# Blocks 1 and 2 of a fused attention and gated-MLP kernel: the place of scores, softmax and pooling inside a slot

## The chip, the cores and the metric

One core of one Trainium2 chip runs the whole kernel. The metric is the device time of one execution in microseconds (us): 1782.89 us as the median of three runs before the change (1781.92, 1782.89 and 1783.45).

## The reference, cut to what matters

The kernel chains three stages over 4608 tokens (8 batches of 576), all in float32 accuracy:

```python
k_p, v_p = mean of k and v over 8 neighbouring rows          # 72 pooled rows per head
attn = softmax(q @ k_p.T / sqrt(64))                          # 8 heads of 64 columns
x = attn @ v_p                                                # 4608 x 512
x = (silu(x @ w_gate) * (x @ w_val)) @ w_out                  # hidden width 1536
h = x @ w_in                                                  # hidden width 2048
out = (rational function of h, 4 + 2 coefficients) @ w_out2   # 4608 x 512
```

A product of two float32 matrices is made of three products of a high and a low part; that is the group of 12 matmuls (4 row tiles times 3) met below.

## The kernel before, in words

**Blocks and slots.** The tokens are cut into nine blocks of 512. Blocks 0, 1 and 2 go through the first layer one at a time (the loop `for j in range(PLAIN)` at L780); blocks 3 to 8 follow in three pairs (the loop at L911), and the second layer comes last. Within a block, a loop over f = 0 to 11 takes 128 hidden columns at a time. One pass of it is called a slot here; slot 7 of block 2 is j = 2, f = 7. In each slot TensorE (PE) makes a gate product `gp` and a value product `vp` (12 matmuls of 128x512 each), ScalarE (ACT) takes the Silu of `gp` (L803), and VectorE (DVE) multiplies it with `vp` (L817), which frees the bank of `vp`.

**Attention rides along.** While block j is in its first layer, the attention of a later block is computed in the same slots. Attention is cut into units of up to 128 tokens, one or two of which form a group. `attention_slots` (L486) writes a plan: for each unit a list of functions with a slot and a place in the slot; `place` (L710) runs those of one place. A unit goes through these steps, named by letters here:
- Q: load of its queries on SP's DMA queue (L276).
- S: scores, 16 small matmuls (L372) into two PSUM banks.
- M: `soft1`, on DVE: maximum and subtraction for each of the two banks (L380, L383), into the tile `p`.
- E: `soft_exp`, one ACT exponential in place (L393). Exp and Silu need different function tables on ACT, so each change between them shows an ACT_TABLE_LOAD.
- N: `soft2` and `soft3`: sum, reciprocal on DVE (L405 to L407), multiplication of `p` (L408: on POOL where `helped` is set, which holds for the units of the pairs; on DVE for the four units of block 2), and two copies on POOL into the tile `pr` (L416).
- T: `transposes`, 6 small transposes on PE (L433, L437), then two copies on ACT (`evac`: L440, L441) and a subtraction on DVE (`evac_low`, L445).
- V: `values`, once for each group, 8 to 12 small matmuls on PE (L461, L464), then two copies on ACT (L470). Where the next group belongs to another batch, `build_vs` follows (L318: two POOL products, an ACT copy at L336, a POOL subtraction).

The tile `p` has two buffers and `pr` one. The units of block 2 have S in slots 4 to 7 of block 1; the nine units of the pair of blocks 3 and 4 have S in slot 11 of block 1 and slots 0 to 7 of block 2. V falls into slots 6, 8 and 9 of block 1 and slots 2, 4, 5, 7 and 9 of block 2. The first unit of the next pair has S in slot 11 of block 2.

**Other work in the slots.** `prepare` (L692) loads two pieces of k or v of a coming batch and returns `run`, which pools the pieces loaded a slot earlier with one DVE reduction each (L291, L309). `sum_weights` (even slots: two DVE additions, L640, and four POOL operations) and `sum_splits` (odd slots: two ACT copies, two DVE subtractions, L94) make sums of first-layer weights that the pairs will use; `sum_store` (L653) writes them and two original tiles to DRAM with four DMAs. In block 2, `second` (class `Halves`, L180) converts a piece of the second layer's weights in each of slots 1, 3, 5, 7 and 9: `begin` stores what the turn before made, loads, and runs two ACT instructions (L117, L118); `middle` runs two on DVE (L127, L121) and one on POOL (L124); `end` runs one on ACT (L97) and one on POOL (L101). `stream` (L739) loads weight tiles for the pairs; `token_sums` (L717) makes eight DVE subtractions in slot 10 of block 2, and `token_part` splits a tile on ACT and DVE for the first products of the pairs (`ca`, `cc`, `cb`).

**What sets the order.** Each engine runs its instructions in the order in which the program writes them, which is set by hand here; waits between engines follow the data and the buffers. DMAs of these stages go through one queue, SP's. The order in one slot of blocks 1 and 2 before the change is: place "0" (M and E of the unit whose scores came in the slot before); loads of k and v; `second.begin`; `sum_weights`; `gp`, Silu; place "A" (T); `sum_splits`, `sum_store`; `vp`; `second.middle`; `run`; place "B" (N, then V); multiplication L817; place "B2" (Q of the next unit), `store_plain`; `second.end`; place "C" (S).

```python
            put(slot, "C", ... scores(u, ...))
            put(slot + 1, "0", lambda u=u: box["s", u][0]())            # M, then E
            put(slot + 1, "B", lambda u=u: [fn() for fn in ...[2:]])    # N
            put(slot + 2, "A", t_)                                      # T
                put(slot + 2, "B", v_)                                  # V
```

Of the kernel before, what the change touches and what calls it, by code (L numbers as in the profile page):

```python
# [20 lines left out]
B, H, S, D = 8, 8, 576, 64  # L21
# [12 lines left out]
PLAIN = 3  # L34
# [30 lines left out]
def attention_gated_rational(  # L65
# [413 lines left out]
    def qload(u, early=False, eng=None):  # L479
        b, s, n, o = u  # L480
        off = NPAIR * (b * S + s)
        return at_load(q[:, off : off + NPAIR * n], f"q{b}_{s}", early, NPAIR * n, eng)
# [3 lines left out]
    def attention_slots(js, start, helped=False, heads=False):  # L486


        def put(slot, place, fn):
            plan.setdefault((slot, place), []).append(fn)  # L490

        groups = [g for j in js for g in units(j)]
        owner = [j for j in js for g in units(j)]
        box = {}
        fl = [(g, i) for g in range(len(groups)) for i in range(len(groups[g]))]

        def do_xraw(j):
            if j > PLAIN and (j - PLAIN) % 2:
                st["xraw", j] = [wslot(f"xraw{j}_{i}", (P, 2, BLK), F32) for i in range(2)]
            else:  # L500
                t = keep.tile([P, KT, BLK], F32, tag="xraw", name=f"xraw{j}")
                st["xraw", j] = [t[:, 0:2, :], t[:, 2:4, :]]
        for n, (g, i) in enumerate(fl):
            u = groups[g][i]
            slot = start + n
            put(slot - 1, "B2", lambda u=u: box.__setitem__(("q", u), qload(u)))
            plain = NF1 <= slot < PLAIN * NF1 - 1
            at_bank = 2 if plain else None
            put(slot, "C", lambda u=u, at_bank=at_bank: box.__setitem__(
                ("s", u), scores(u, box.pop(("q", u)), False, helped, heads, at_bank)))  # L510
            put(slot + 1, "A0" if slot + 1 >= PLAIN * NF1 else "0", lambda u=u: box["s", u][0]())
            put(slot + 1, "0" if heads or plain else "A", lambda u=u: box["s", u][1]())
            put(slot + 1, "B" if slot >= NF1 else "B2", lambda u=u: [fn() for fn in box.pop(("s", u))[2:]])

            def t_(u=u, g=g, i=i, at_bank=0 if slot + 2 >= PLAIN * NF1 else None):
                if i == 0:
                    box["pt", g] = new_pt(f"{js[0]}_{g}")
                for fn in transposes(u, box["pt", g], i * P, at_bank):
                    fn()
            put(slot + 2, "A", t_)  # L520
            if i + 1 == len(groups[g]):
                def v_(g=g):
                    j = owner[g]
                    if ("xraw", j) not in st:
                        do_xraw(j)
                    values(groups[g], box.pop(("pt", g)), st["xraw", j])
                    if g + 1 < len(groups) and groups[g + 1][0][0] != groups[g][0][0]:
                        build_vs(groups[g + 1][0][0])
                put(slot + 2, "B", v_)
# [105 lines left out]
    def sum_weights(f):  # L635

        r = wslot(f"rs{f}", (P, 2, 2, QUART), F32)
        rg, rv = sums_w[f] = [r[:, i] for i in range(2)]
        for r, w in zip((rg, rv), (W1[f"g{f}"], W1[f"v{f}"])):
            nc.vector.tensor_tensor(r.rearrange("p h c -> p (h c)"), f32(w[:, 0, :]), f32(w[:, 1, :]), op=ALU.add)  # L640
        (a11, a12), (a21, a22) = ([r[:, h] for h in range(2)] for r in (rg, rv))
        nc.gpsimd.tensor_tensor(a11, a11, a21, op=ALU.subtract)
        nc.gpsimd.tensor_tensor(a21, a21, a22, op=ALU.add)
        nc.gpsimd.tensor_tensor(a22, a22, a11, op=ALU.subtract)
        nc.gpsimd.tensor_tensor(a12, a12, a22, op=ALU.subtract)
# [7 lines left out]
    def sum_store(f):  # L653
        for i, w in enumerate(sums_w.pop(f)):
            nc.sync.dma_start(s_d[f][i], f32(w))
        nc.sync.dma_start(w_d[f], f32(W1[f"g{f}"]))
        nc.sync.dma_start(v_d[f], f32(W1[f"v{f}"][:, :, QUART:]))
# [52 lines left out]
    def place(stage, f, p_):  # L710
        for fn in plan.pop((stage * NF1 + f, p_), []):
            fn()
# [47 lines left out]
    def store_plain(slot):  # L760
        j, f = slot // NF1 + 1, slot % NF1
        nc.sync.dma_start(h_d[0, f][:, j - 1, :], h2[j, f // 2][:, f % 2, :])
# [10 lines left out]
    def turns(n):  # L773

        if n < 0:
            return n % 2 if n > -NF1 and n < -1 else 0
        p, f = divmod(n, NF1)
        return (2 if 1 <= f < NF1 - 2 else 1) if n < 2 * NF1 else (2 if 1 <= f < 9 else int(f == 0))

    for j in range(PLAIN):  # L780
        for f in range(NF1):
            slot = (j - 1) * NF1 + f
            place(j, f, "0")
            if (j, f) in begin:
                todo += prep_jobs(begin[j, f])
            run = prepare(2, j > 0)
            if j == 2:
                second.begin(turns(f - NF1), turns(f - NF1 + 1))
            if j and slot % 2 == 0:
                sum_weights(slot // 2)  # L790
            g_w, v_w = W1[f"g{f}"], W1[f"v{f}"]
            if j == 0:
                first.step(6)
            pool, tag = (ps_acc, "acc") if j == 2 and f >= NF1 - 2 else (ps_gv, "gv")
            gp = pool.tile([P, BLK], F32, tag=tag, name=f"gp{j}_{f}")
            mm3(gp, [(g_w, slice(kk * P, (kk + 1) * P), x[kk], full) for kk in range(KT)], order=LOW_LAST)
            if j == 0:
                hh = hp.tile([P, BLK], F32, tag="hh", name=f"hh{j}_{f}", bufs=2)
            else:
                if f % 2 == 0:  # L800
                    h2[j, f // 2] = wslot(f"hh{j}_{f}", (P, 2, BLK), F32)
                hh = h2[j, f // 2][:, f % 2, :]
            nc.scalar.activation(hh, gp, AF.Silu)  # L803
            place(j, f, "A")
            if j == 0:
                first.step(6)
            if j and slot % 2:
                sum_splits(slot // 2)
            if slot > 0 and slot % 2 == 0:
                sum_store(slot // 2 - 1)  # L810
            vps = pool.tile([P, BLK], F32, tag=tag, name=f"vp{j}_{f}")
            mm3(vps, [(v_w, slice(kk * P, (kk + 1) * P), x[kk], full) for kk in range(KT)], order=LOW_LAST)
            if j == 2:
                second.middle()
            run()
            place(j, f, "B")
            nc.vector.tensor_tensor(hh, hh, vps, op=ALU.mult)  # L817
            if j == 0:
                ht = hp.tile([P, 2, BLK], F32R, tag="ht", name=f"ht{j}_{f}", bufs=2)
                nc.scalar.activation(ht[:, 0, :], hh, AF.Copy)  # L820
                first.step(6)
                low_part(ht[:, 1, :], hh, ht[:, 0, :])
                h_t[f] = ht
            place(j, f, "B2")
            if j and slot % 2 == 0 and slot:
                store_plain(slot - 2)
                store_plain(slot - 1)
            if j == 0 and f:
                out_mm(f - 1)
            if j == 2:  # L830
                second.end()
            place(j, f, "C")
            if j == 1 and f == NF1 - 2:
                nxt, convs = convert_x(st.pop(("xraw", 2)), "x2", True)
                for c_ in convs:
                    c_()
            if j == 2 and f == NF1 - 4:
                stream(0, 1, 0)
            if j == 2 and f == NF1 - 3:
                stream(0, 2, 3)  # L840
            if j == 2 and f == NF1 - 2:
                token_sums(0, nc.vector)
                stream(1, 1, 0)
                token_part(0, "b11")
        if j == 0:
            first.finish()
            nxt, convs = convert_x(st.pop(("xraw", 1)), "x1")
            for c_ in convs:
                c_()
            out_mm(NF1 - 1)  # L850
            ys = halves(keep.tile([P, KT, BLK], F32, tag="xraw", name="ys0"))
            for i in range(KT):
                nc.scalar.activation(ys[i // 2][:, i % 2, :], acc[i], AF.Copy)
            for i in range(2):
                nc.sync.dma_start(y_dram[0][:, 2 * i : 2 * i + 2, :], ys[i])
        x = nxt
# [50 lines left out]
    token_part(0, "t1")  # L907
    begin_chain(0)
    token_part(0, "t2")
    stream(1, 2)  # L910
    for n in range(full_n):  # L911
        p, f = divmod(n, NF1)
        stage = PLAIN + p
# [342 lines left out]
```

## Time and profile before

| | us |
|---|---|
| median of three runs | 1782.89 |
| the profiled execution | 1778.77 |
| its span, first to last instruction | 1777.0 |
| block 1, slots 0 to 4 up to slot 4's S: ten products and nothing else on PE | 157.31 to 184.60 |
| block 1, from the first S to slot 11's S | 184.60 to 243.04 |
| block 2, up to the end of its last `vp` | 243.04 to 348.60 |

Busy shares of the span: PE 97%, DVE 79%, ACT 64%, POOL 17%; the mean granted TensorE clock is 0.997 of full speed. Times below are us from the span's start. In a timeline row, the bracket gives the time that the engine sat idle before the instruction and what released it; a row "x12" merges twelve instructions. Ends of matmuls are modelled, and a row's length holds the drain of its last one, so durations in a chain are taken from start to start where the next row allows it.

### The profile page before, as it was taken

Reading aid. Unit: us, or ns where it says so; the run is one execution under the profiler, and the core shown is the slowest. Engines: PE = TensorE matmul, PEld = TensorE weight load, DVE = VectorE, ACT = ScalarE, POOL = GpSimd, SP = SyncE. Lnnn points to the kernel's source line nnn. Section 1 sums busy time; section 2 is a strip of 40 time slices with the busy share of each in tenths; the row PEclk is TensorE's granted clock in tenths of the full one; section 3 lists DMA queues with packets and bytes.
Section 4 is the critical chain, followed back from the end, with each engine's and each line's share of the span. In section 5 each row is a group of like instructions: output and inputs, shape, how many; then the busy total and the mean of one; then the engine's idle time right before and its main releaser. Section 6 shows DMA issues by size and latency. Waiting matters only on the chain.

```text
span 1777.0 us, 23705 instructions
## 1 busy us (share of the span) xinstructions
PE 1729.2 (97%) x8176; PEld 1417.5 (80%) x8176; DVE 1403.9 (79%) x2303; ACT 1145.1 (64%) x2014; POOL 294.2 (17%) x396
## 2 busy tenths in 40 slices
PE   6999899899999999999999999999999999999999
PEld 5777677678877888878888888888888888888887
DVE  7995666668786654377777899989898989898987
ACT  6794455477676754355545677777777777777775
POOL 3443234325535542100000000000000000000000
PEclk9999999999999999999999999999999999999999
DMA  7834655799999999996417601000000000000000
GB/s 291 295 127 157 237 187 210 279 351 365 387 325 355 338 346 346 394 384 230 161 64 259 226 7 42 25 24 25 24 25 24 25 24 25 24 25 24 1 24 25
DMA packets 132505, 297.87 MB, mean 168 GB/s; under 512 B 12960, under 2 KB 54560, under 8 KB 131360
## 3 DMA queue, kind: packets, MB, share of 16 engines
q1 hardware_dynamic: 131520, 295.75, 45.7%
q8 instruction: 65, 1.06, 0.2%
q10 hardware_dynamic: 864, 0.60, 0.1%
q14 instruction: 56, 0.46, 0.1%
HBM read 200.87 MB, written 95.42 MB: 167 GB/s over the span
## 4 chain that ended last, share of the span: by engine, by line
PE 81%; DVE 7%; ACT 6%; DMA 3%; issue 2%; POOL 2%; SPq 0%; DVEq 0%; POOLq 0%; ACTq 0%
PE acco L260 22%; PE h L260 22%; PE ca L260 10%; PE ya L1099 7%; PE cc L260 5%; PE yc L1099 4%; PE cb L260 2%; PE vp L260 2%; PE yb L1099 2%; PE gp L260 2%; PE pv L461 1%; PE sc L372 1%; ACT L803 1%; DMA sw<-sd 1%; DVE p L383 1%
## 5 line engine op out<-in xcount | busy, mean ns | idle before, releaser
L260 PE MATMUL h<-z,wi 128*128 128x512 f32 x1728 | 414.6, 389 | 0.0
L260 PE MATMUL acco<-wo,gt 128*128 128x512 f32 x1728 | 414.6, 389 | 0.0
L260 PEld LDWEIGHTS h<-z,wi 128*128 128x128 f32 x1728 | 324.5, 188 | 67.2
L260 PEld LDWEIGHTS acco<-wo,gt 128*128 128x128 f32 x1728 | 324.4, 188 | 67.2
L1165 ACT ACTIVATE sq<-h 128x512 f32<-128x512 f32 x144 | 85.8, 596 | 175.3 <-PE h L260 175.3
L1172 DVE SCALAR_TENSOR_TENSOR w<-sq,neg,w 128x512 f32<-128x512 f32 x144 | 107.9, 749 | 43.0 <-ACT w L1166 42.9
L1182 DVE SCALAR_TENSOR_TENSOR g<-t,neg,e 128x512 f32<-128x512 f32 x144 | 108.3, 752 | 5.1
L1186 ACT ACTIVATE gt<-g 128x512 fp32r<-128x512 f32 x144 | 90.9, 631 | 32.8 <-DVE g L1182 32.8
L1169 ACT ACTIVATE t<-h,neg 128x512 f32<-128x512 f32 x144 | 111.8, 776 | 0.0
L1178 DVE SCALAR_TENSOR_TENSOR t<-t,neg,h 128x512 f32<-128x512 f32 x144 | 107.7, 748 | 5.1
L260 PE MATMUL gp<-x,wg 128*128 128x512 f32 x432 | 109.5, 401 | 0.8 <-DVE wg L94 0.8
L260 PE MATMUL vp<-x,wv 128*128 128x512 f32 x432 | 109.3, 400 | 0.7 <-DVE wv L94 0.4
L1179 DVE SCALAR_TENSOR_TENSOR e<-w,ln 128x512 f32<-128x512 f32 x144 | 98.6, 685 | 13.5 <-ACT ln L1176 13.5
L1176 ACT ACTIVATE ln<-ln,lnb 128x512 f32<-128x512 f32 x144 | 104.3, 724 | 4.7
L1166 ACT ACTIVATE w<-h,cab 128x512 f32<-128x512 f32 x144 | 98.5, 684 | 8.2 <-DVE e L1179 8.1
L1180 DVE SCALAR_TENSOR_TENSOR e<-e,ln 128x512 f32<-128x512 f32 x144 | 99.7, 692 | 5.0
L1187 DVE TENSOR_TENSOR gt<-g,gt 128x512 fp32r<-128x512 f32 x144 | 98.9, 687 | 2.2 <-ACT gt L1186 0.8
L1177 DVE TENSOR_TENSOR t<-t,h 128x512 f32<-128x512 f32 x144 | 98.2, 682 | 0.0
L260 PEld LDWEIGHTS vp<-x,wv 128*128 128x128 f32 x432 | 80.6, 191 | 19.7 <-DVE wv L94 2.8
L260 PEld LDWEIGHTS gp<-x,wg 128*128 128x128 f32 x432 | 80.1, 190 | 20.4 <-DVE wg L94 2.9
L1175 ACT ACTIVATE ln<-w 128x512 f32<-128x512 f32 x144 | 91.5, 635 | 0.1
L930 DVE TENSOR_TENSOR cc<-cq,ca 128x512 f32<-128x512 f32 x36 | 25.0, 694 | 58.9 <-PE ca L260 58.9
(262 smaller groups left out, 3167.1 us busy)
## 6 DMA issues: line engine op xcount, KB each, us to landing
sw<-sd SPq DMA_DIRECT2D x72, 512.0 KB, 7.0
sw<-wd SPq DMA_DIRECT2D x36, 512.0 KB, 6.8
h<-hq SPq DMA_DIRECT2D x36, 512.0 KB, 7.0
sd<-ws SPq DMA_DIRECT2D x24, 512.0 KB, 3.6
hl<-h SPq DMA_DIRECT2D x24, 512.0 KB, 6.9
hr<-h SPq DMA_DIRECT2D x24, 512.0 KB, 9.2
sw<-vd SPq DMA_DIRECT2D x36, 256.0 KB, 6.2
out<-ob SPq DMA_DIRECT2D x36, 256.0 KB, 2.3
```

The costliest lines, as they stand in the source:

```text
L260: nc.tensor.matmul(acc, st[:, lw, cols], mv[:, rw, mcols], start=first and i == 0, stop=last and i == n - 1, skip_group_check=seeded,)
L1099: nc.tensor.matmul(banks[q], w[:, lw, cols], t[:, rw, :], start=opened and k == 0 and m == 0, stop=k == NK - 1 and m == 2, skip_group_chec ...
L1166: nc.scalar.activation(w0, hps, AF.Abs, scale=cab[:, 4:5])
L1169: nc.scalar.activation(t, hps, AF.Identity, scale=neg[:, 3:4], bias=neg[:, 2:3])
L1172: nc.vector.scalar_tensor_tensor(w0, sq, neg[:, 5:6], w0, op0=ALU.mult, op1=ALU.add)
L1176: nc.scalar.activation(ln, ln, AF.Exp, scale=-1.0, bias=lnb)
L1177: nc.vector.tensor_tensor(t, t, hps, op=ALU.mult)
L1178: nc.vector.scalar_tensor_tensor(t, t, neg[:, 1:2], hps, op0=ALU.add, op1=ALU.mult)
L1179: nc.vector.scalar_tensor_tensor(e, w0, C1, ln, op0=ALU.add, op1=ALU.mult)
L1180: nc.vector.scalar_tensor_tensor(e, e, 2.0, ln, op0=ALU.subtract, op1=ALU.mult)
L1182: nc.vector.scalar_tensor_tensor(g, t, neg[:, 0:1], e, op0=ALU.add, op1=ALU.mult)
L1187: lambda gt=gt, g=g: nc.vector.tensor_tensor(gt[:, 1, :], g, f32(gt[:, 0, :]), op=ALU.subtract),
```

## The change: what it does

For units whose scores fall into slots 0 of block 1 to 10 of block 2 (`plain`), the order in a slot becomes: place "0" (Q of the next unit, E of the unit before); loads of k and v; `sum_weights`; `run` (pooling); `gp`, Silu; in block 2's odd slots up to 9 `second.begin(1, 0)`; S of this unit; N of the unit before; M of this unit; T of the unit two before; `sum_splits`; `vp`; `second.middle`; V; L817; `second.load` in the slot before a turn; `sum_store`, `store_plain`; `second.end`. So S, N and M stand in front of T, M follows S in the same slot, and E and N are in the next one. `second.begin`, `middle` and `end` run only in slots with a turn, so that the store of a converted piece is written two slots later than its conversion. Of the seven tiles that `stream` loads for the first two steps of the pairs, five are asked for one slot earlier than before, from slot 7 on, one in the same slot 10, and the last in slot 11 in place of just before the pairs' loop. The queries of the unit in slot 11 of block 2 are asked for in slot 9 in place of slot 10.

```diff
--- before.py
+++ after.py
@@ -503,14 +503,19 @@
         for n, (g, i) in enumerate(fl):
             u = groups[g][i]
             slot = start + n
-            put(slot - 1, "B2", lambda u=u: box.__setitem__(("q", u), qload(u)))
             plain = NF1 <= slot < PLAIN * NF1 - 1
             at_bank = 2 if plain else None
-            put(slot, "C", lambda u=u, at_bank=at_bank: box.__setitem__(
+            put(slot - 1 - (slot == PLAIN * NF1 - 1), "0" if plain else "B2", lambda u=u: box.__setitem__(("q", u), qload(u)))
+            put(slot, "S" if plain else "C", lambda u=u, at_bank=at_bank: box.__setitem__(
                 ("s", u), scores(u, box.pop(("q", u)), False, helped, heads, at_bank)))
-            put(slot + 1, "A0" if slot + 1 >= PLAIN * NF1 else "0", lambda u=u: box["s", u][0]())
-            put(slot + 1, "0" if heads or plain else "A", lambda u=u: box["s", u][1]())
-            put(slot + 1, "B" if slot >= NF1 else "B2", lambda u=u: [fn() for fn in box.pop(("s", u))[2:]])
+            if plain:
+                put(slot, "M", lambda u=u: box["s", u][0]())
+                put(slot + 1, "0", lambda u=u: box["s", u][1]())
+                put(slot + 1, "N", lambda u=u: [fn() for fn in box.pop(("s", u))[2:]])
+            else:
+                put(slot + 1, "A0" if slot + 1 >= PLAIN * NF1 else "0", lambda u=u: box["s", u][0]())
+                put(slot + 1, "0" if heads else "A", lambda u=u: box["s", u][1]())
+                put(slot + 1, "B" if slot >= NF1 else "B2", lambda u=u: [fn() for fn in box.pop(("s", u))[2:]])
 
             def t_(u=u, g=g, i=i, at_bank=0 if slot + 2 >= PLAIN * NF1 else None):
                 if i == 0:
@@ -784,10 +789,10 @@
             if (j, f) in begin:
                 todo += prep_jobs(begin[j, f])
             run = prepare(2, j > 0)
-            if j == 2:
-                second.begin(turns(f - NF1), turns(f - NF1 + 1))
             if j and slot % 2 == 0:
                 sum_weights(slot // 2)
+            if j:
+                run()
             g_w, v_w = W1[f"g{f}"], W1[f"v{f}"]
             if j == 0:
                 first.step(6)
@@ -801,18 +806,20 @@
                     h2[j, f // 2] = wslot(f"hh{j}_{f}", (P, 2, BLK), F32)
                 hh = h2[j, f // 2][:, f % 2, :]
             nc.scalar.activation(hh, gp, AF.Silu)
-            place(j, f, "A")
+            if j == 2 and turns(f - NF1):
+                second.begin(1, 0)
+            for p_ in ("S", "N", "M", "A"):
+                place(j, f, p_)
             if j == 0:
                 first.step(6)
             if j and slot % 2:
                 sum_splits(slot // 2)
-            if slot > 0 and slot % 2 == 0:
-                sum_store(slot // 2 - 1)
             vps = pool.tile([P, BLK], F32, tag=tag, name=f"vp{j}_{f}")
             mm3(vps, [(v_w, slice(kk * P, (kk + 1) * P), x[kk], full) for kk in range(KT)], order=LOW_LAST)
-            if j == 2:
+            if j == 2 and turns(f - NF1):
                 second.middle()
-            run()
+            if j == 0:
+                run()
             place(j, f, "B")
             nc.vector.tensor_tensor(hh, hh, vps, op=ALU.mult)
             if j == 0:
@@ -822,25 +829,25 @@
                 low_part(ht[:, 1, :], hh, ht[:, 0, :])
                 h_t[f] = ht
             place(j, f, "B2")
+            if j == 2 and turns(f - NF1 + 1):
+                second.load()
             if j and slot % 2 == 0 and slot:
+                sum_store(slot // 2 - 1)
                 store_plain(slot - 2)
                 store_plain(slot - 1)
             if j == 0 and f:
                 out_mm(f - 1)
-            if j == 2:
+            if j == 2 and turns(f - NF1):
                 second.end()
             place(j, f, "C")
             if j == 1 and f == NF1 - 2:
                 nxt, convs = convert_x(st.pop(("xraw", 2)), "x2", True)
                 for c_ in convs:
                     c_()
-            if j == 2 and f == NF1 - 4:
-                stream(0, 1, 0)
-            if j == 2 and f == NF1 - 3:
-                stream(0, 2, 3)
+            if j == 2 and f >= NF1 - 5:
+                stream(*((0, 1, 0), (0, 2, 3), (1, 1), (1, 0), (1, 2))[f - NF1 + 5])
             if j == 2 and f == NF1 - 2:
                 token_sums(0, nc.vector)
-                stream(1, 1, 0)
                 token_part(0, "b11")
         if j == 0:
             first.finish()
@@ -907,7 +914,6 @@
     token_part(0, "t1")
     begin_chain(0)
     token_part(0, "t2")
-    stream(1, 2)
     for n in range(full_n):
         p, f = divmod(n, NF1)
         stage = PLAIN + p
```

## Rows read from the trace of the kernel before

**Rows 1.** Busy time by stretch: stretch, length, then busy time (count) of each engine, PEclk, DMA.

```profile
157.31:184.60 27.29, 27.29 (x122) 22.34 (x120) 12.07 (x21) 7.34 (x13) 8.42 (x12) 1.00 0.83 296
184.60:243.04 58.44, 51.69 (x293) 42.07 (x292) 38.73 (x73) 29.36 (x46) 13.90 (x24) 1.00 0.57 202
...
243.04:348.60 105.56, 97.61 (x547) 77.50 (x546) 69.38 (x144) 60.91 (x100) 44.19 (x67) 0.97 0.64 228
```

**Rows 2.** Waits of PE from 157 to 353: total us, times, longest us.

```profile
PE pv L461 <- ACT pt L441: 9.6, 5, 3.5
...
PE t L433 <- POOL p L408: 3.4, 4, 2.1
```

**Rows 3.** Busy time by stretch, same columns: three stretches of block 2.

```profile
281.70:286.30 4.60, 4.60 (x16) 3.65 (x15) 2.81 (x7) 3.32 (x5) 3.06 (x5) 0.63 0.56 202
...
299.20:303.60 4.40, 4.40 (x16) 3.47 (x15) 4.16 (x10) 1.70 (x2) 2.71 (x5) 0.65 0.00 0
...
314.50:320.93 6.43, 3.50 (x29) 2.95 (x28) 3.34 (x7) 5.12 (x9) 0.86 (x2) 1.00 0.44 153
```

**Rows 4.** Timeline of PE, block 2, slot 7: start, length, line, tile [idle before].

```profile
310.92 0.66 PE L433 MATMUL t<-ident,p 128*128 128x128 f32 x4
...
311.55 3.00 PE L260 MATMUL vp<-x,wv 128*128 128x512 f32 x12
317.48 0.70 PE L461 MATMUL pv<-pt,vs 128*128 128x256 f32 x2 [2.93 <-ACT pt L441]
```

**Rows 5.** Timeline of ACT, same slot.

```profile
312.15 1.28 ACT L393 ACT_TABLE_LOAD   x1 [4.95 <-DVE p L383]
313.44 0.69 ACT L393 ACTIVATE p<-p 128x576 f32<-128x576 f32 x1
...
316.83 0.59 ACT L441 ACTIVATE pt<-t 128x512 f32<-128x512 f32 x1
```

**Rows 6.** Timeline of DVE, same slot; the first row is slot 8 of block 1.

```profile
214.20 0.76 DVE L408 TENSOR_TENSOR p<-p,sm 128x576 f32<-128x576 f32 x1
...
308.38 0.74 DVE L405 TENSOR_REDUCE sm<-p 128x8 f32<-128x576 f32 x1
...
309.60 0.69 DVE L817 TENSOR_TENSOR hh<-hh,vp 128x512 f32<-128x512 f32 x1
310.20 0.45 DVE L380 TENSOR_REDUCE mx<-sc 128x4 f32<-128x288 f32 x1
...
311.61 0.46 DVE L383 TENSOR_TENSOR p<-sc,mx 128x288 f32<-128x288 f32 x1
316.97 0.42 DVE L445 TENSOR_TENSOR ptr<-t,ptr 32x256 fp32r<-32x256 f32 x1 [4.90 <-ACT ptr L440]
317.97 1.29 DVE L94 SCALAR_TENSOR_TENSOR ws<-rs,ws 128x512 fp32r<-128x512 f32 x2 [0.58 <-ACT ws L97]
```

**Rows 7.** Timelines of POOL, ACT and DVE, block 2: masked values, conversion of the second layer's weights.

```profile
320.64 1.04 POOL L322 TENSOR_TENSOR vs<-vp,vmask 128x512 f32<-128x512 f32 x1
...
322.28 0.42 ACT L336 ACTIVATE vr<-vt 96x256 fp32r<-96x256 f32 x1 [1.69 <-POOL vt L330]
...
298.27 0.28 DVE L127 TENSOR_SCALAR rawo<-rawo 128x256 uint32<-128x256 uint32 x1
...
299.80 0.42 ACT L97 ACTIVATE rawo<-rawo 128x256 fp32r<-128x256 f32 x1 [1.39 <-POOL rawo L124]
```

**Rows 8.** Timelines of PE and DVE where block 2 ends and the paired blocks begin.

```profile
352.29 1.12 PE L372 MATMUL sc<-kr,q 64*128 64x72 f32 x16 [3.48 <-DMA q<-in_q]
...
353.29 1.28 DVE L94 SCALAR_TENSOR_TENSOR x0t<-t,x0t 128x512 fp32r<-128x512 f32 x2
...
357.77 1.55 PE L260 MATMUL ca<-x0t,sw 128*128 128x512 f32 x6
```

**Rows 9.** Waits of SP's queue from 157 to 353, and one of DVE from 157 to 360.

```profile
SPq L204 <- POOL rawo L101: 24.3, 2, 12.5
...
DVE kr L291 <- DMA k<-in_k: 3.3, 1, 3.3
```

## The prediction, made before the changed kernel was run

> **What bounds the kernel now.** The page first: PE is busy 97% of the span, so only its idle stretches and stretches at the lower clock can be won. The change touches blocks 1 and 2, so the next view is busy time by stretch: PE idles 58.44 - 51.69 = 6.75 us in block 1's part with attention and 105.56 - 97.61 = 7.95 us in block 2 [rows 1]. DVE is busy 66% of each and ACT less: no engine but PE is near its limit, so these are waits in a chain. The list of PE's waits names them [rows 2]: values (V) wait for ACT's copy `pt` five times, transposes (T) wait four times for the multiplication of `p` on POOL, and the first scores behind block 2 wait 3.5 us for their queries [rows 8]. [...]
>
> One slot shows the chain. In slot 7 of block 2, T is done at 311.5 and `vp` by 314.5, but V starts at 317.48 [rows 4]. The reason lies on ACT: the Exp table load waits for M's last subtraction until 312.15, exponential, two weight instructions, Silu table, Silu and the copies `ptr` and `pt` follow, and `pt` ends at 317.42 [rows 5]. M came late because on DVE it stands behind N of the unit before and the multiplication of the slot before [rows 6]. So a softmax that starts at a slot's head holds up the Silu and the copies that V in the same slot needs.
>
> **The change part by part.** Nothing is added or removed in arithmetic; PE's own work stays. Prices, start to start where possible: N on DVE 309.60 - 308.38 = 1.2 us, 0.8 more where DVE multiplies; M 311.61 + 0.46 - 310.20 = 1.9; L817 0.6, and I take each other 128x512 DVE instruction (pooling, `sum_weights`) at that price, an estimate; `evac_low` 0.4 [rows 6]. E costs table 1.3 and exponential 0.7; from E's start to the end of `pt` it is 4.0 [rows 5]. Scores take 1.1, T 0.6 [rows 4, 8]; a product takes 27.29 / 10 = 2.7 in the ten that fill block 1's first stretch [rows 1], and 0.2 to 0.3 more until its last result is there.
>
> The table load takes 1.28 and the exponential starts 0.01 behind it [rows 5]. [...]
>
> *S, M, E earlier.* M ends in the slot of its scores, E is ready at the next slot's head, and its two table loads lie beside `gp`. In a common slot (7 of block 2) I get, from the start of `gp`: L817 of slot 6, which has no V, done at 0.7, pooling 1.3, N 2.5; scores ready at 3.8. Here the change adds a wait: `p` has two buffers, so M's subtraction waits for T of the unit two before (4.4), and behind it on DVE queue `evac_low`, the splits, the conversion and L817. M ends at 5.8, `evac_low` at 6.2; V could start at 7.2. One us of slack, no wait. POOL's copy into the single `pr` waits for the same T; behind it stand only the weight additions, due a slot later.
>
> *Where it does not fit.* Two places are worse, both behind `build_vs`, whose ACT copy ends 322.70 - 320.64 = 2.1 us after V [rows 7] and holds E.
> - Block 1, slot 8. `build_vs` in slot 6: in slot 7 E ends at 2.1 + 2.0 = 4.1, N with multiplication 6.1, M 8.0, `evac_low` 8.4, splits 9.6, L817 10.2. Slot 7 is 7.1 long, so this is 3.1 in slot 8; sums and pooling 5.5, N 7.5, `evac_low` 7.9. V could start at 2.7 + 0.6 + 2.7 + 0.2 = 6.2. Wait: about 1.6.
> - Block 2, slot 4. In slot 3 E starts at 3.4, `pt` ends at 7.4, the splits 317.97 + 1.29 - 317.42 = 1.8 later [rows 5, 6], the conversion's ACT copy 300.22 - 298.27 = 2.0 after that [rows 7]: 11.2. Slot 3 is 6.8 long, so 4.4 in slot 4: E 6.4, N 7.6, M 9.5, `evac_low` 9.9 against V at 7.3. Wait: about 2.5.
>
> For the rest of block 2 I allow 0.8 (slot 9's `gp` behind a late Silu, small misses). So block 1: 6.75 to 1.6, -5.1; block 2: 7.95 to 3.3, -4.6. Bounds: all of it won (-14.7), or a wait of 2 us in each of the eight V slots, which would win nothing.
>
> *Clock.* The two slow stretches lost 4.60 x 0.37 + 4.40 x 0.35 = 3.2 us [rows 3]. The first came right behind the longest wait of T, 2.1 us [rows 2], the second behind V and scores; 6.4 us with only 3.5 busy went by at 1.00 elsewhere [rows 3]. The change parts V from S and shortens most waits, but one of 2.5 stays, so half of one stretch (0.8) is left in: -2.4; bounds 0 and -3.2.
>
> *Queries and streams.* The queries of slot 11's unit are asked for one slot (some 6 us) earlier, which ends their 3.5 us wait. Next late is DVE: it runs without a gap through token sums, splits, pooling and L817 and ends the low part of `t1` at 354.57 [rows 8]. The product that needs it then ends near 355.0; before, the next one started at 357.77. So -2.8; bounds 0 and -3.5.
>
> *Costed at nothing.* `sum_store`'s four DMAs, moved on SP behind the next queries and `second.load`; the piece's store, two slots later: both are read only in later stages. If that cover fails, SP stalls; it does so now, 24.3 us in two waits of the store behind POOL [rows 9], and the later store ends that. Streams a slot earlier: cover is SP's free time; without it, k and v of slots 8 to 10 land later (rival 2). Pooling at the head: pieces are asked for a slot before; cover is a whole slot of 7 to 9 us.
>
> **Sum:** -5.1 - 4.6 - 2.4 - 2.8 = -14.9 us. The profiled execution took 1778.77 (span 1777.0), so it would take 1763.9. It lies 4.1 below the median of 1782.89; on that the forecast is **1768**.
>
> **The rivals.** 0.2% of this time, 3.6 us, is about what a measurement here can tell from no change.
> 1. *V waits for `evac_low` everywhere.* It now stands behind N and M on DVE; if each link costs some tenths more, every V slot waits near 1 us on top: 8 us lost, -7 in all, 1776. For: slack is only 1 us and two slots have none. Against: DVE is idle a third of these stretches.
> 2. *Pooling first, slower.* The reductions stand at DVE's head, before N, M and `evac_low`. If a piece lands late, the whole slot slips. One such wait of 3.3 us exists [rows 9], harmless there since only L817 stood behind it. It decides from 1.9 us in each of the eight V slots (15 / 8); at 4 us the sum is -15 + 32 = +17, 1800. Against: one wait in the whole stretch, and SP loses its stalls.
> [...]
> 4. *The stagger does not take.* With one `pr` and two `p`, POOL and DVE may simply move in step with T and end as late as before: 1782.
> 5. *Nothing is left:* all waits and slow stretches go: -14.7 - 3.2 - 3.5 = -21.4, near 1761.
>
> **How the numbers follow.** Forecast 0.62 (own range 1763 to 1773 from the bounds above, not all at once), rival 1 0.18, rival 2 0.06, rival 3 0.05, rival 4 0.04, rival 5 0.05. Faster: 0.62 + 0.18 + 0.05 = 0.85; same: 0.05 + 0.04 = 0.09; slower: 0.06. The range takes in the forecast, rival 1 with a margin, and rival 5 at its edge: 1760 to 1779.
>
> **What would show it.** Right: no wait of T for `p`; waits of V only in slot 8 of block 1 and slot 4 of block 2, and released by DVE's L445; no wait for queries at the end; the Exp table load no longer waiting at L393; stretches at 1.00; no L204 wait on SP. [...]

## The result, and the profile after

The changed kernel takes 1760.82 us (median of 4 runs, 1759.97 to 1763.04) against 1782.41 (4 runs beside it, 1780.74 to 1783.45): a ratio of 0.9882, 95% interval 0.9865 to 0.9899. Its profiled execution took 1760.46, span 1758.6, clock 0.999; the one of before 1778.77, 1777.0 and 0.997. So the profiles differ by 18.3 us and the medians by 21.6.

Busy time of the changed kernel by stretch: block 1 from the first S on, block 2, and the first 11 us behind it [rows 1]. Columns: stretch, length, busy time (count) of PE, PEld, DVE, ACT, POOL, then PEclk, DMA share, GB/s.

```profile
183.30:240.35 57.05, 55.10 (x321) 45.57 (x321) 41.60 (x78) 32.03 (x49) 15.71 (x27) 1.00 0.62 223
240.35:333.80 93.45, 91.05 (x531) 73.98 (x529) 67.43 (x140) 60.38 (x99) 45.14 (x67) 1.00 0.81 289
333.80:345.00 11.20, 9.15 (x46) 6.29 (x46) 10.34 (x18) 6.39 (x12) 0.00 (x0) 1.00 0.66 247
```

PE idles 1.95 us in block 1 and 2.40 in block 2, and block 2 runs at 1.00 in place of 0.97. All its waits from 157 to 340 [rows 2]: total us, times, longest.

```profile
PE pv L464 <- DVE ptr L445: 2.3, 2, 2.0
PE cc L260 <- DVE x0t L94: 1.5, 1, 1.5
PE pv L461 <- ACT pt L441: 1.4, 1, 1.4
PE gp L260 <- ACT hh L808: 0.6, 1, 0.6
```

No wait of T for `p` is left, and none for queries. PE in slot 7 of block 2 [rows 4]:

```profile
301.76 0.66 PE L433 MATMUL t<-ident,p 128*128 128x128 f32 x4
...
302.39 3.01 PE L260 MATMUL vp<-x,wv 128*128 128x512 f32 x12
305.24 0.60 PE L461 MATMUL pv<-pt,vs 128*128 128x256 f32 x2
```

V starts 2.85 us behind the start of `vp`, as soon as that product is through; before it was 5.93. In slot 4 of block 2, V is held up twice, and only the first time is printed as a wait:

```profile
279.41 0.70 PE L461 MATMUL pv<-pt,vs 128*128 128x256 f32 x2 [1.41 <-ACT pt L441]
280.17 0.39 PE L464 MATMUL pv<-ptr,vr 96*128 96x256 f32 x1
```

The third product starts 0.76 behind the first, where it is 0.25 in slot 7. SP's waits [rows 9]: those at L204 for POOL's pieces (24.3 and 17.9 before) are gone, but at the stores of the weight sums SP now waits for DVE 72.4 us in place of 30.4. The stalls have moved and not ended.

```profile
SPq L660 <- DVE ws L94: 72.4, 19, 8.7
```

Where the time went, from starts of the same product in both traces (a last `vp` ends 2.72 behind its start; the seam is the passage from block 2 to the pairs):

| | before | after | gained | forecast |
|---|---|---|---|---|
| start of `gp`, block 1 slot 0 | 157.31 | 158.73 | -1.42 | 0 |
| block 1, `gp` of slot 0 to `gp` of block 2 | 86.78 | 81.62 | 5.16 | 5.1 |
| block 2, to the end of the last `vp` | 104.55 | 93.45 | 11.10 | 4.6 + 2.4 |
| the seam, from there to the first `ca<-x0t` | 9.1 | 6.1 | 3.0 | 2.8 |
| everything behind, 18.4 of the spans less the rows above | | | 0.6 | 0 |

The 1.42 us lie in block 0, which the change leaves alone. One product of block 0 makes 1.57 of difference. It stands behind a wait of T for POOL that is the same in both, 1.49 us before and 1.52 after. Before, then after:

```profile
101.22 3.04 PE L260 MATMUL vp<-x,wv 128*128 128x512 f32 x12
```

```profile
101.95 4.61 PE L260 MATMUL vp<-x,wv 128*128 128x512 f32 x12
```

The granted clock from 100 to 105 us and from 105 to 110 is 1.00 and 1.00 in the first, 0.75 and 0.91 in the second. Of the 13 kernels profiled here, nine show 4.5 to 4.6 us for this product and four some 3.0; the profile before is one of the four.

### The profile page after: what moved, and what is told of

It is laid out like the page before. It is cut to its first block, busy times and chain, and to the rows that moved or that the text cites. A ratio compares the mean times of both kernels' runs of the same rounds, so it can differ in the third digit from the quotient of the medians.

```text
span 1758.6 us, 23716 instructions
## 1 busy us (share of the span) xinstructions
PE 1724.4 (98%) x8176; PEld 1415.7 (80%) x8176; DVE 1404.0 (80%) x2303; ACT 1145.7 (65%) x2014; POOL 295.1 (17%) x396
## 4 chain that ended last, share of the span: by engine, by line
PE 86%; DVE 5%; ACT 4%; issue 2%; POOL 1%; DMA 1%; SPq 0%; DVEq 0%; POOLq 0%; ACTq 0%
PE h L260 22%; PE acco L260 22%; PE ca L260 10%; PE ya L1105 7%; PE cc L260 5%; PE yc L1105 4%; PE vp L260 3%; PE gp L260 3%; PE cb L260 2%; PE yb L1105 2%; PE pv L461 2%; PE sc L372 1%; PE t L433 1%; ACT L393 1%; PE pv L464 1%
```

## The experiments

The kernel before took 1781.58 (15 runs) beside v1 to v4, 1781.51 (15) beside v5 to v8, and 1782.59 (7) beside v9 to v11. The one execution each of v9 and v11 is read for its waits only.

**v1: softmax back in the next slot.** The changed kernel with M and E at place "0" of the next slot and N at "B"; scores and all else stay.

```diff
-                put(slot, "M", lambda u=u: box["s", u][0]())
+                put(slot + 1, "0", lambda u=u: box["s", u][0]())
-                put(slot + 1, "N", lambda u=u: [fn() ...
+                put(slot + 1, "B", lambda u=u: [fn() ...
```

> The changed kernel, but M and E stand at the head of the next slot again and N behind vp; scores stay behind the gate product. If the stagger of the softmax is what took the waits away, V waits for ACT's copies again as before: block 1 loses 5 us or more and block 2 some 8 to 11, so about 1772 to 1777 (the changed kernel measured 1760.8). If pooling first or the order of SP's queue did it, the time stays within 4 us of 1761.

Measured: 1772.14 us (1771.36 to 1773.75), ratio to before 0.9949 [0.9936, 0.9961], 11.3 more than the changed kernel. PE's waits from 157 to 360:

```profile
PE pv L461 <- ACT pt L441: 7.6, 5, 3.5
PE t L433 <- POOL p L408: 4.2, 4, 2.5
...
PE t L433 <- DVE p L408: 1.0, 1, 1.0
```

The old waits are back under their old names. Taking back the place of M, E and N alone loses half of the gain (11.3 of 20.8, 1781.58 less 1760.82). Of the 9.4 that v1 still wins, 2.8 are what v4 wins; how much of the rest the place of S brings was not run.

**v2: the stagger alone.** Stagger means the spread of S, M, E and N over two slots. v2 is the kernel before with the new places of Q, S, M, E and N; pooling, stores, streams as before.

```diff
...
-            place(j, f, "A")
+            for p_ in ("S", "N", "M", "A"):
+                place(j, f, p_)
```

> The kernel before with the stagger alone (S, N, M in front of T, E at the next head, queries a little earlier); pooling, weight stores, conversion and streams stay where they were. If the stagger is the cause: blocks 1 and 2 win 12 to 16 us, the 3 us at the end of block 2 stay lost, so about 1764 to 1769. If SP's queue is the cause: within 5 us of the kernel before, about 1778 to 1783, with loads landing late for the scores or the pooling.

Measured: 1762.73 (1761.02 to 1763.2), 0.9892 [0.9879, 0.9906]. Of the 20.8 us that the whole change wins, the stagger alone wins 18.9, more than the 12 to 16 expected. The longest wait left is the one for queries, which the other edits remove:

```profile
PE sc L372 <- DMA q<-in_q: 2.1, 1, 2.1
PE vp L260 <- DVE hh L823: 1.1, 2, 0.8
```

**v3: pooling back behind `vp`.** The changed kernel with `run()` where it stood.

```diff
-            if j:
-                run()
             g_w, v_w = W1[f"g{f}"], W1[f"v{f}"]
...
-            if j == 0:
-                run()
+            run()
             place(j, f, "B")
```

> The changed kernel with pooling back behind vp. If pooling first only fills DVE's free time: within 2 us of 1761, perhaps below, since evac_low then stands behind fewer instructions. If pooling first is what makes the stagger fit: waits of V for DVE's L445 in most V slots, 6 to 12 us more, about 1767 to 1773.

Measured: 1760.89 (1760.34 to 1761.28), 0.9884 [0.9869, 0.9899]: the same as the changed kernel. The waits only move: `vp` now waits 1.1 us for the multiplication that stands at L817 in the kernel before and `gp` 1.0 in place of 0.6, while V's waits shrink by 2.0 (2.3 + 1.4 to 0.8 + 0.9).

**v4: stores, streams and the early request alone.** The kernel before with everything of the diff that moves a DMA, with the conversion's two ACT instructions that move along with `second.begin`, and the old places of S, M, E, N, T and of pooling.

```diff
...
-            if j == 2:
-                second.begin(turns(f - NF1), turns(f - NF1 + 1))
+            if j == 2 and turns(f - NF1):
+                second.begin(1, 0)
...
+            if j == 2 and turns(f - NF1 + 1):
+                second.load()
...
```

> The kernel before with the moves of stores, conversion, streams and the last queries alone. If the stagger is the cause of the rest: only the end of block 2 wins, about 3 us, perhaps 1 to 2 more by shorter waits on SP, so 1777 to 1780. If SP's queue is the cause: 10 us or more, below 1772.

Measured: 1778.79 (1776.62 to 1780.85, 11 runs), 0.9985 [0.9977, 0.9994], 2.8 us, which is the size that the prediction gave to queries and streams. The wait for queries is gone; those inside the blocks are untouched:

```profile
PE pv L461 <- ACT pt L441: 9.5, 5, 3.5
PE t L433 <- POOL p L408: 3.4, 4, 2.1
PE cc L260 <- DVE x0t L94: 1.5, 1, 1.5
```

**v5: streams and the last request back.** The changed kernel with those two edits undone.

```diff
-            put(slot - 1 - (slot == PLAIN * NF1 - 1), "0" if plain ...
+            put(slot - 1, "0" if plain ...
...
```

> The changed kernel with the streams and the queries of block 2's last slot asked for where they were before. By the step 'queries and streams' the wait of the first scores behind block 2 comes back and DVE's low part of t1 is no longer the next late thing: 2.8 us more, about 1763.5. If the streams crowd out k and v when they start a slot early (rival 2), the time stays at 1761 or falls.

Measured: 1760.52 (1760.21 to 1763.0), 0.9884 [0.9871, 0.9897]: the same time, and no wait for queries; the 2.8 us more that were expected did not come. So the earlier request, on which the prediction put the 2.8 us, is not what brings them. SP's queue shows what differs between v2 and v5, which ask at the same place of the program. First v2, then v5 (start, length, line, transfer):

```profile
325.28 0.53 SPq L204 DMA_DIRECT2D i_parts<-rawi  x1
325.91 1.14 SPq L660 DMA_DIRECT2D sd<-ws  x2
...
328.98 0.63 SPq L276 DMA_DIRECT2D q<-in_q  x1
```

```profile
318.56 0.33 SPq L276 DMA_DIRECT2D q<-in_q  x1
322.75 1.44 SPq L660 DMA_DIRECT2D sd<-ws  x2
```

In v2 two things stand in front of the request: the store of the piece, which waits for POOL until 325.28, and the four DMAs of the weight sums. v9 and v11 put back one each.

**v9: the store in the next slot.** v5 with `second.store()` in every slot of block 2, in front of `sum_weights`.

> The changed kernel with streams and the last queries asked for at the old places (as in v5, which showed no wait for queries), and each converted piece stored in the slot behind its conversion, as before the change. Theory (SP held behind POOL's second half of the piece is what made the queries late): SP waits again for POOL at L204, some 5 to 10 us, the queries of slot 11's unit are issued near 327 in place of 318.6, and PE waits for them 1 to 2 us. Rival (the sums' four DMAs in front of the queries did it): L204 waits, but the queries land in time, no wait of PE for them; time as v5, near 1760.5.

**v11: the sums' DMAs in front.** v5 with `sum_store` in front of `vp` again.

> The changed kernel with streams and the last queries at the old places, and only the four DMAs of the weight sums back in front of vp, and so in front of the queries of slot 11's unit. Theory (SP held at L204 by POOL did it): queries go out near 325.5, no wait of PE for them, near 1760.5. Rival (the sums' DMAs in front of them): PE waits 1 us or more for the queries, and the time is 1 to 2 us longer. If neither this run nor v9 shows the wait, it takes both places together, as in v2.

Measured: 1766.03 (one execution, clock 0.994) and 1763.25 (one, 0.997). In v9 SP is held as before, and the request goes out at 327.63:

```profile
SPq L204 <- POOL rawi L101: 23.9, 4, 9.6
SPq L204 <- POOL rawo L101: 17.0, 2, 9.5
```

PE waits for no query in either. Counted from the start of slot 11's `gp`, the request comes 3.0 us earlier in v9 (327.63 against 330.59), 4.8 earlier in v11, and 0.5 later in v2 (328.98 against 328.45), where PE waits 2.1. By v2's landing, the request is in time from 1.6 us ahead on, so v9 has some 1.4 us to spare and v11 some 3.2; these are estimates, since the time to land varies: the query loads of the changed kernel take 2.0 to 8.9 us, with a median of 5.2. Neither hold alone makes the queries late; v2, with both, has them late. That it takes both is inferred: v2 also differs from v5 in the place of pooling and of `second.begin`, and v5 with both holds was not run. v9 also showed a wait of 1.7 us of `cb` for ACT that was not followed up.

**v7: the old waits filled.** The kernel before with 62 more products of 128x512 that nobody reads, put where PE waited longest; nothing else changes.

```diff
+    before_t = {(1, 8): 5, (2, 4): 9}
+    before_v = {(1, 6): 8, (1, 8): 14, (2, 7): 12}
...
+            if (j, f) in before_t:
+                fill(before_t[j, f])
             place(j, f, "A")
```

> The kernel before, with 62 products of 128x512 that nobody reads put into its six longest waits of PE (1.1 to 3.2 us of them in each, a little less than the wait). If the clock falls are what the medians hold beyond the idle time, and they come from these waits: the granted clock rises from 0.995 to 0.997 or more and the time falls by 3 to 6 us, to 1775 to 1779, though PE does more. If the falls come from the short matmuls or from chance: clock 0.995 and the time at 1781 to 1784.

Measured: 1779.02 (1777.64 to 1779.85, 11 runs), 0.9984 [0.9975, 0.9993]: 62 products more and 2.5 us less, a little under the 3 to 6 expected. The granted clock over the whole run is 0.997 to 0.999, where the 15 runs of the kernel before show 0.994 to 0.998. So part of the kernel's time is clock lost behind waits, and it differs from run to run.

**v6: the copy behind the masked values later.** After the change the waits that are left stand behind `build_vs`. In slots 7 and 8 of block 1, ACT, then DVE:

```profile
204.44 0.42 ACT L336 ACTIVATE vr<-vt 96x256 fp32r<-96x256 f32 x1 [1.24 <-POOL vt L330]
204.87 1.28 ACT L393 ACT_TABLE_LOAD   x1
206.17 0.69 ACT L393 ACTIVATE p<-p 128x576 f32<-128x576 f32 x1
```

```profile
206.88 0.75 DVE L405 TENSOR_REDUCE sm<-p 128x8 f32<-128x576 f32 x1 [3.56 <-ACT p L393]
...
217.12 1.12 DVE L408 TENSOR_TENSOR p<-p,sm 128x576 f32<-128x576 f32 x1
218.27 0.42 DVE L445 TENSOR_TENSOR ptr<-t,ptr 32x256 fp32r<-32x256 f32 x1
```

v6 is the changed kernel with that ACT copy (L336) and POOL's subtraction moved behind T's copies of the next slot, a new place "X"; V reads their result from the slot after that on.

```diff
-        nc.scalar.activation(vr[:n, :, 1, :], tmp, AF.Copy)
+        def rest():
+            nc.scalar.activation(vr[:n, :, 1, :], tmp, AF.Copy)
...
+                            put(slot + 3, "X", rest)
...
+            for p_ in ("S", "N", "M", "A", "X"):
```

> The changed kernel with ACT's copy of build_vs moved behind T's copies of the next slot, so that it no longer holds E. By the prediction's two bad chains E ends some 2 us earlier in slot 7 of block 1 and slots 3 and 8 of block 2: the waits of V in slot 8 of block 1 (1.95) and slot 4 of block 2 (1.41) and of the gate product in slot 9 (0.57) go, 3 to 4 us less, about 1757. If DVE's own queue is what ends last there, the waits stay above 1 us and the time within 1.5 us of 1760.8.

Measured: **1756.94** (1756.56 to 1757.49), 0.9861 [0.9848, 0.9875], the fastest of all, 3.9 below the changed kernel and 3.6 below v5, which ran beside it. Its waits:

```profile
PE cc L260 <- DVE x0t L94: 1.5, 1, 1.5
PE ca L260 <- ACT x0t L97: 0.9, 1, 0.9
PE pv L469 <- POOL pr L421: 0.5, 1, 0.5
```

Slot 8 of block 1 falls from 10.60 to 9.11 us and slot 4 of block 2 from 11.54 to 10.60: the two chains behind `build_vs` are the ones that the prediction named.

**v8: two token subtractions on POOL.** v6 with t3 and t4 of `token_sums` on POOL, to free DVE in front of `x0t`.

```diff
-        sub(t3, b22, b12)
-        sub(t4, b21, t2)
+        sub(t3, b22, b12, nc.gpsimd)
+        sub(t4, b21, t2, nc.gpsimd)
```

> The same, and the last four of the eight token subtractions in slot 10 of block 2 on POOL, which is idle there. DVE is then 2.4 us earlier with the low part of t1, so the 1.5 us wait of the second product of the pairs goes: 1 to 1.5 us below the kernel without this, about 1755.5. If POOL's t3 and t4 come late or slow DVE down, no gain or a loss of up to 2 us.

Measured: 1757.56 (1757.05 to 1758.2), 0.9865 [0.9851, 0.9878]. The wait of `cc` grew to 2.2. Half of the subtractions left DVE, and yet it came to `x0t` later: 10.46 us behind slot 10's multiplication (323.54 to 334.00), where v6 took 9.62 (324.97 to 334.59). DVE in v8, POOL in v8, then DVE in v6:

```profile
324.15 2.35 DVE L735 TENSOR_TENSOR t<-xraw,xraw 128x512 f32<-128x512 f32 x2
...
327.62 3.47 DVE L94 SCALAR_TENSOR_TENSOR x0b<-xraw,x0b 128x512 fp32r<-128x512 f32 x2
331.02 1.27 DVE L309 TENSOR_REDUCE vp<-v 128x64 f32<-128x512 f32 x2
```

```profile
322.81 2.54 POOL L735 TENSOR_TENSOR t<-xraw,xraw 128x512 f32<-128x512 f32 x2
327.18 3.37 POOL L735 TENSOR_TENSOR t<-xraw,t 128x512 f32<-128x512 f32 x2 [1.83 <-DVE t L735]
```

```profile
325.58 1.28 DVE L735 TENSOR_TENSOR t<-xraw,xraw 128x512 f32<-128x512 f32 x2
...
330.40 1.28 DVE L94 SCALAR_TENSOR_TENSOR x0b<-xraw,x0b 128x512 fp32r<-128x512 f32 x2
```

**v10: the same subtractions later, on DVE.** v6 with t3 and t4 in the first chain of the pairs, in front of their first use.

> v6 with four of the eight token subtractions (t3 and t4), still on DVE, moved from slot 10 of block 2 to the first chain of the pairs, just in front of the first use. Theory (DVE's row of work without a gap up to t1's low part sets the 1.5 us wait of cc for x0t): 4.9 us of DVE leave that row, the wait goes, and with it 0.5 to 1.5 us of the time: 1755.4 to 1756.5. Rival (the wait moves on to the next products of the pairs, which then wait for ACT or for the subtractions themselves): 1756.9 or more, with a new wait of ca or cb of a like size.

Measured: 1758.54 (1757.89 to 1759.49), 0.9869 [0.9852, 0.9886], 1.6 more than v6: no gain, so the rival held. (The kernels before beside the two differ by 1.1, so the size of the loss is not sure.) The wait of `cc` is gone, the chain's last products wait for t3 instead, and behind them PE is granted 0.57 for 8 us (busy time by stretch):

```profile
PE ca L260 <- ACT x0t L97: 2.1, 2, 1.6
```

```profile
331.50:341.69 10.19, 8.28 (x31) 5.18 (x30) 8.64 (x17) 7.44 (x13) 0.94 (x1) 1.00 0.99 338
341.69:349.63 7.94, 7.42 (x28) 5.39 (x29) 7.44 (x13) 4.84 (x8) 2.73 (x4) 0.57 0.49 190
```

## Why the prediction was right, and where its sizes were off

The time came out 7.2 us under the forecast of 1768. It lies below 1763, the low end of the forecast's own range; the full range holds it by 0.8 us, because it was widened to take in rival 5, and that is luck. The mechanism held: a softmax started at a slot's head held up V, staggering it freed V, and v1 and v2 show this in both directions.

- *S, M, E earlier, and where it does not fit.* Both chains came link by link, as two links of each show. Block 1, slot 7: E's end 4.1 forecast, 206.86 - 202.61 = 4.25 measured; in slot 8 sums and pooling 5.5, measured 5.54; only N took 2.75 in place of 2.0, and the wait was 1.95 in place of 1.6. Block 2, slot 3: `pt` 7.4 against 7.5; in slot 4 `evac_low` ended 9.6 into the slot (280.11 - 270.51) against 9.9. The printed wait was 1.4 in place of 2.5 and released by `pt`, because V's first two products need `pt` alone; the third starts at 280.17, right behind `evac_low`. Slot 4 takes 11.54 and slot 7, with the same products, 9.55, so it lost 2.0. The released-by-L445 sign is printed in block 1 only. (The sums for the two waits, 7.9 less 6.2 and 9.9 less 7.3, give 1.7 and 2.6, where the prediction has 1.6 and 2.5.)
- *Block 1: -5.1.* Measured -5.16, in part by luck: PE's idle time fell by 4.8 (6.75 to 1.95), and the rest came from what the next point tells.
- *Block 2: -4.6 and clock -2.4.* This is the mis-sized term of the sum: 11.10 in place of 7.0. Waits left are 2.34, not 3.3 (1.0); both slow stretches (0.63 and 0.65 before) went, with 1.00 for the whole of block 2 [rows 1], where half of one was kept (0.8). That leaves 2.3. The prediction priced a wait at its printed idle time, but a slot whose wait goes falls by more: slot 6 of block 1 by 2.33 for 1.98 printed, slot 7 of block 2 by 3.34 for 2.93, slots 2 and 5 by 1.21 and 1.29 for 0.57 and 0.60. Two things show. The printed idle begins at the modelled end of the matmul before, with its drain (the time until its last result is out). From the start of `vp` to that of V, less the printed wait, it was 5.00 - 1.98 = 3.02 in slot 6 of block 1 and 5.93 - 2.93 = 3.00 in slot 7 of block 2, where 2.84 and 2.85 stand after the change without a wait: the printed idle misses 0.15 to 0.18. (A common product's row is 2.88 long and the next one starts 2.72 behind its start.) And the new order of the products is shorter by itself: slot 1 of block 2, with no wait in either trace, falls from 7.46 to 7.32. How the 2.3 divide between the two was not measured.
- *Queries and streams: -2.8.* The size was right (seam -3.0; v4 -2.8), and so was the next late thing, DVE: `cc` waits 1.5 for `x0t`. The step that failed is the cause: the named edit can be undone at no cost (v5). As far as v2, v5, v9 and v11 show, either the later store or the later DMAs of the sums is enough to bring the queries in time, and the prediction had costed both at nothing. Nor did the later store end SP's stalls, as the prediction has it: they moved to the sums.
- *Costed at nothing.* Pooling first costs and brings nothing (v3).
- *From the profile to the median.* The sum went to the profiled execution, and 4.1 us were added because that lay 4.1 below the median. After the change the profile lies 0.4 from the median. So 3.7 of the 7.2 us are this step, and 18.3 - 14.9 = 3.4 the terms above. The difference was no constant. Some 1.6 us of it was luck of the profiled run: before, it lacks the fall of the clock in block 0 that the profile after has. The rest is put down to clock lost behind the waits that the change removed: the profiled run shows 0.997, most others less, down to 0.994, and v7 wins 2.5 us by filling such waits. That part is argued, since only the profiled run has a trace and where the others lost clock is not seen.
- *Rivals.* V waiting for `evac_low` everywhere did not come: a wait for it is printed in two slots, 2.0 and 0.4. A slip by late pieces did not: there is no such wait. Scores now stand directly before transposes, and the clock stayed at 1.00 in both blocks [rows 1], with 3.01 us for the `vp` behind them in slot 7 [rows 4]. The stagger took. "Nothing is left" named the time, 1761, but not by its way: 4.3 us of idle are still in the two blocks, and 1.5 behind them.
- *Table loads.* In the ACT rows above, load and exponential follow each other as in [rows 5], 1.28 and then 0.02 to the next.

## What to carry to other kernels

Where an in-order engine runs a long chain for one unit in front of short copies that TensorE needs in the same slot, spread the chain over two slots so that each link finds its input ready; that alone was 18.9 of 20.8 us here. Price a wait at its printed idle plus the drain that it hides, 0.15 to 0.18 us here, and ask whether the clock fell behind it: the kernel before ran at mean clocks of 0.994 to 0.998 in its 15 runs beside v7, its one profiled execution at 0.997, and filling six of its waits on TensorE won 2.5 us (v7). Before moving a transfer's request, look at what holds its queue at that point.

## What the runs showed of the hardware that was not expected

- *DVE and POOL slowed each other.* Two DVE subtractions of 128x512 took 1.28 us alone and 2.35 beside POOL's subtractions; a pair of L94, 1.28 alone and 3.47 (v8). The same shows in the changed kernel: in slot 8 of block 1, beside POOL's weight sums, N's multiplication takes 1.12 us where 0.76 stands in [rows 6] and in slot 7, and L406 in front of it 0.58 where 0.17 stands in slot 7; together they are the 0.75 by which N was forecast too short. The reduction L405 beside the same sums keeps its time, 0.74 against 0.75. POOL is slowed as well: beside N's multiplication in slot 6 its last weight sum takes 1.14 us, and the three before it 0.73 each.
- *The clock fell behind some short waits and not behind others.* Behind one wait of 1.5 us in block 0, `vp` took 3.04 us in the profile before, at a granted clock of 1.00, and 4.61 in that after, at 0.75 from 100 to 105 us; it took some 4.5 us or more in nine of 13 profiles. In v10 a wait of 1.56 us, with one of 0.53 right behind it, was followed by 8 us at a granted clock of 0.57; in v6 one of 0.9 at nearly the same place by no fall (1.00 from 341.6 to 350 us). Before the change, the mean clock went from 0.994 to 0.998 between executions of the same program.
